# One core, attention followed by a leaky-ReLU MLP: another order of the first units of work and of three middle groups

## The chip, the cores and the metric

The kernel runs on one core of a Trainium2 chip. The metric is the device time of one execution in microseconds (us), the median of several runs. The engines are named as in the profile: PE (matrix products), DVE, ACT and POOL (elementwise work), and SP, which issues most DMAs. The profile comes from one execution, so its numbers are set against that execution's own time.

## The reference

```python
# q, k, v: (4, 8, 768, 64) float32; lam: (8,); w_in: (512, 2048) float64; w_out: (2048, 512) float64
for b in range(12):                       # blocks of 64 tokens, with a running state per head
    intra = (qb @ kb.T * Dmask) @ vb      # Dmask[i, j] = lam ** (i - j) for j <= i
    inter = (qb * lam_pow) @ kv_state
    out[block] = intra + inter
    kv_state = lam_block * kv_state + (kb * rev_pow).T @ vb
x = out as (3072, 512)
h = x @ w_in
return maximum(0.01 * h, h) @ w_out       # (3072, 512) float32
```

## The kernel before

**Precision.** Every float32 operand of a large product is split into a high, a low and a middle part (`xh`, `xl`, `xm`; `wh`, `wl`, `wm`), and a product is three passes over these parts. The weights arrive as 64-bit floats and are converted on the chip.

**Units of work.** The tokens are cut into 24 chunks of 128, and six groups of four chunks. The 2048 columns of `w_in` are cut into eight blocks `p` of 256. The list `seq` (L1030) names the work in order:

- `("a", c)`, `("b", c)`, `("r", c)`: the attention of chunk c. A round `("r", c)` (`round_of`, L556) issues on PE the transposes of chunk c+2 (until chunk 9), the outputs of chunk c, and the scores of chunk c+1; then ACT writes `xh` of chunk c, and DVE its `xl` and `xm`. DVE also masks the next scores (L478) and updates the state (L485), with POOL scaling it in between (L488). It loads k of chunk c+2, q too until chunk 9, and v. These loads of a chunk go into two buffers taken in turn, so that the loads of chunk 9 wait for the last use of those of chunk 7.
- `("wi", p)`: the conversion of block p of `w_in` (`w_in`, L650). It makes two loads of 512 KB into a ring of three buffers (`raws`), three ACT and two DVE instructions for each (L614 to L621) into one staging tile `w32`, and then `wh`, `wl`, `wm` (L629, L632, L647).
- `("up", g, p, lo, hi)`: the first layer for group g and block p (`up`, L755), limited to the chunks lo to hi where they are given. A whole unit is 24 matmuls of 512 columns in two halves, each 4 with `wh`, 4 with `wl`, and 4 with `wm`. Between the second and the third pass ACT scales the bank (L786), and after the third it writes the result to `gs` (L791).
- `("ls",)` and `("lt",)`: loads of k and q for the chunks from 10 on in strips, 16 DMAs each, those of q issued by POOL (L400).

From group 2 on, `steps` (L1038) lists the eight units of each group in the order `ORDER`, with a round after every second unit and a conversion of `w_out` after each. The last group, 5, takes the blocks from 0 to 7. After that come the products with `w_out`, most of them in a Strassen form; this part begins at about 337 us.

**What sets the order on the engines.** A planner (`Plan`, L37) goes through all operations with assumed durations and writes each engine's queue. It always takes the operation that can start first, and among those that can start at the same time the one with the lower rank; the rank is the place in `seq` (L1093), so a move in `seq` moves the priority of every operation of that unit on each engine and DMA queue. The hardware then follows the written queues in order.

The place in `seq` also fixes buffers. The halves of the units take three PSUM banks in turn:

```python
kb = ("b10", "b2")[n_b % 2] if n_b < 0 else ("b10", "b11", "b2")[(n_b + TURN_B) % 3]   # L777
```

A half waits until the half that had its bank before it, by the order of `seq`, is written out by ACT. The `gs` buffers (L760) alternate from unit to unit in the same way. For the fifth to the seventh unit of `seq` the banks are b2 and b10, b11 and b2, b10 and b11.

Some units (p below 2 in groups 0 and 1, below 6 in groups 2 and 3, below 4 in groups 4 and 5) add and subtract parts of their result on DVE (`sums`, L821) for the Strassen form. They use a scratch strip in `raws` when p is even, one in `lows` when p is odd (`spare`, L810). The others only store their result.

Of the kernel before, what the change touches and what calls it, by code (L numbers as in the profile page):

```python
# [166 lines left out]
def kernel(  # L167
# [856 lines left out]
    def add_banks(d, s):  # L1024
        for i in range(2):
# [3 lines left out]

    seq = [  # L1030
# [5 lines left out]
    nxt, n_out, begin = 3 * GC, 0, len(seq)  # L1036
    ORDER = [2, 1, 4, 3, 0, 5, 7, 6]
    steps = [(g, p) for g in range(2, NG) for p in (ORDER if g < NG - 1 else range(NP))]  # L1038

    def key_of(g, p):  # L1040
# [132 lines left out]
```

## Time and profile before

| | |
|---|---|
| median of 3 runs | 598.83 us (598.42 to 599.55) |
| profiled execution, its own time | 598.96 us |
| its span | 597.2 us |
| busy: PE, DVE, ACT, POOL | 584.0, 433.4, 306.2, 134.8 us |
| granted PE clock | 1.00 |

The profiled execution lies 0.13 us over the median, and its span 1.76 us under its own time. Busy time is an average over stages that differ: the first 100 us hold the conversions of `w_in`, the rounds until 297 us the attention, and the rest the second layer.

### The profile page before, as it was taken

How to read it: one execution, taken by the hardware profiler on the slowest of the kernel's cores; microseconds unless marked ns; L12 is line 12 of the kernel's file. 1: busy time of each engine (PE TensorE's matmuls, PEld its weight loads, DVE VectorE, ACT ScalarE, POOL GpSimd, SP SyncE). 2: the span in 40 equal slices, each digit the busy share in tenths (PEclk: the TensorE clock that was granted, in tenths of full speed). 3: DMA queues.
4: the chain of work that ended last, by engine and by line, in shares of the span. 5: the costliest groups of instructions: out<-in, count | busy, mean ns of one | idle time of the engine just before them, and what ended most of it. 6: DMA issues, size and time to landing. Idle time of an engine off the chain costs nothing.

```text
span 597.2 us, 13439 instructions
## 1 busy us (share of the span) xinstructions
PE 584.0 (98%) x5324; PEld 481.7 (81%) x5324; DVE 433.4 (73%) x596; ACT 306.2 (51%) x478; POOL 134.8 (23%) x170
## 2 busy tenths in 40 slices
PE   7899999999999999999999999999999999999997
PEld 5678888888888888888788878888888888888886
DVE  5899986525677464675269989886698887788972
ACT  4688883445555555565588783433343332335410
POOL 2654494616436436431000000000000000000000
PEclk9999999999999999999999999999999999999999
DMA  8899766978989989997889765534868668869644
GB/s 208 224 292 250 239 175 156 228 206 211 264 240 269 242 268 254 261 294 225 260 265 300 239 201 185 187 124 154 236 200 253 195 218 251 281 201 294 186 121 88
DMA packets 171199, 133.55 MB, mean 224 GB/s; under 512 B 101376, under 2 KB 147200, under 8 KB 171136
## 3 DMA queue, kind: packets, MB, share of 16 engines
q1 hardware_dynamic: 155376, 123.24, 70.8%
q10 hardware_dynamic: 13200, 5.77, 3.7%
q0 software_dynamic: 2560, 3.68, 2.4%
q8 instruction: 42, 0.69, 0.5%
q14 instruction: 21, 0.17, 0.1%
HBM read 85.99 MB, written 46.66 MB: 222 GB/s over the span
## 4 chain that ended last, share of the span: by engine, by line
PE 90%; DVE 5%; DMA 2%; ACT 1%; issue 0%; POOL 0%; SPq 0%
PE b L767 42%; PE po L909 13%; PE b L909 12%; PE psc L909 11%; PE pt L909 4%; PE po L339 3%; PE psc L339 3%; DMA attb<-in_q_dram 2%; DVE w L620 1%; DVE wm L647 1%; DVE w L621 1%; DMA attb<-in_k_dram 1%; PE pt L429 1%; DVE wl L632 0%; PE po L429 0%
## 5 line engine op out<-in xcount | busy, mean ns | idle before, releaser
L767 PE MATMUL b<-xh,wh 128*128 128x512 f32 (+2 forms) x392 | 103.5, 387 | 0.9 <-ACT xh L533 0.8
L767 PE MATMUL b<-xl,wl 128*128 128x512 f32 (+2 forms) x392 | 103.4, 387 | 0.7 <-DVE xl L534 0.6
L767 PE MATMUL b<-xm,wm 128*128 128x512 f32 (+2 forms) x392 | 103.9, 393 | 0.0
L882 ACT ACTIVATE xh<-xm 128x1024 fp32r<-128x1024 f32 x51 | 54.1, 1062 | 82.8 <-DMA xm<-b 50.3
L767 PEld LDWEIGHTS b<-xh,wh 128*128 128x128 f32 x392 | 72.8, 188 | 16.8 <-ACT xh L533 0.9
L767 PEld LDWEIGHTS b<-xl,wl 128*128 128x128 f32 x392 | 72.8, 188 | 15.9 <-DVE xl L534 1.0
L767 PEld LDWEIGHTS b<-xm,wm 128*128 128x128 f32 x392 | 71.3, 188 | 14.8
L786 ACT ACTIVATE b<-b 128x512 f32<-128x512 f32 (+2 forms) x97 | 56.2, 582 | 49.0 <-PE b L767 48.5
L791 ACT ACTIVATE gs<-b 128x512 f32<-128x512 f32 (+2 forms) x97 | 57.1, 593 | 44.0 <-PE b L767 38.2
L885 DVE SCALAR_TENSOR_TENSOR xl<-xm,xh 128x1024 fp32r<-128x1024 f32 x51 | 62.2, 1219 | 16.2 <-ACT xh L882 15.8
L889 DVE SCALAR_TENSOR_TENSOR xm<-xl,xh 128x1024 fp32r<-128x1024 f32 x52 | 63.7, 1225 | 4.0
L478 DVE TENSOR_TENSOR att<-psc,att 128x512 f32<-128x512 f32 x24 | 16.5, 688 | 38.9 <-PE psc L339 38.9
L488 POOL TENSOR_TENSOR att<-att 128x256 f32<-128x256 f32 x40 | 33.9, 847 | 42.2 <-DVE att L485 41.3
L400 POOL DMA_DIRECT2D attb<-in_q_dram x64 | 39.4, 622 | 4.9 <-DVE att L409 4.3
L449 POOL TENSOR_TENSOR att<-att 128x512 f32<-128x512 f32 (+1 forms) x20 | 24.8, 1240 | 53.7 <-PE po L339 18.9
L445 POOL TENSOR_TENSOR attb<-attb,att 128x512 f32<-128x512 f32 (+1 forms) x23 | 27.7, 1202 | 37.4 <-DMA attb<-in_k_dram 16.3
L909 PE MATMUL psc<-xm,wm 128*128 128x512 f32 x80 | 31.2, 391 | 0.8 <-DVE xm L889 0.8
L621 DVE CUSTOM_DVE_ANT_0 w<-w,lows 128x1024 uint16<-128x1024 uint16 x32 | 26.3, 822 | 7.3 <-ACT lows L618 5.9
L909 PE MATMUL psc<-xl,wl 128*128 128x512 f32 x80 | 31.2, 390 | 0.0
L909 PE MATMUL psc<-xh,wh 128*128 128x512 f32 x80 | 31.1, 389 | 0.0
L620 DVE TENSOR_SCALAR w<-w 128x512 int32<-128x512 int32 x32 | 22.1, 692 | 8.7 <-ACT w L614 8.5
L616 ACT ACTIVATE lows<-raws 128x512 uint16<-128x512 uint32 x32 | 25.2, 786 | 1.1 <-DVE w L621 1.1
(189 smaller groups left out, 1102.6 us busy)
## 6 DMA issues: line engine op xcount, KB each, us to landing
xm<-b SPq DMA_DIRECT2D x35, 512.0 KB, 4.3
b<-gs SPq DMA_DIRECT2D x24, 512.0 KB, 3.7
g<-gs SPq DMA_DIRECT2D x23, 512.0 KB, 3.6
xm<-g SPq DMA_DIRECT2D x17, 512.0 KB, 4.3
raws<-in_moe_w_in_dram SPq DMA_DIRECT2D x16, 512.0 KB, 5.2
raws<-in_moe_w_out_dram SPq DMA_DIRECT2D x16, 512.0 KB, 5.0
attb<-in_k_dram SPq DMA_DIRECT2D x48, 128.0 KB, 4.2
attb<-in_v_dram SPq DMA_DIRECT2D x24, 256.0 KB, 4.5
```

Of the source, the lines that this page charges most:

```text
L339: nc.tensor.matmul(dst[HALF[cols]], lhsT=lhsT[HALF[rows]], rhs=rhs[HALF[rows]], start=start, stop=True, skip_group_check=True)
L400: (move if nm == "k" else carry)(0.55 if nm == "k" else QSL, lambda o=o, z=z, e=nc.sync if nm == "k" else nc.gpsimd: e.dma_start(out=o.rea ...
L488: add("POOL", 0.7, lambda new=new, j=j: nc.gpsimd.tensor_tensor(state[(j + 1) % 4], new, _bc(lam_c, 2, D), op=ALU.mult), [f"st{j % 4}", "f ...
L620: add("DVE", 0.42, lambda: nc.vector.tensor_scalar(d, d, 3, None, op0=ALU.logical_shift_left), [], [key])
L621: add("DVE", 1.0, lambda: nc.vector.tensor_tensor(d, d, low, op=ALU.add), [kl], [key])
L767: nc.tensor.matmul(dst, lhsT=w[z][:, kk * 2 * P + f * P:kk * 2 * P + (f + 1) * P], rhs=x[z][:, kk, toks], start=start and kk == 0, stop=kk ...
L786: add("ACT", ns, lambda b=b: nc.scalar.activation(out=b, in_=b, func=AF.Copy, bias=0.0, scale=S + 1.0), [], [kb], rank=-1.5)
L791: add("ACT", t, lambda o=o, x=s_: nc.scalar.activation(out=o, in_=x, func=AF.Prelu, bias=0.0, scale=(1.0 + 1.0 / S) / (WS * U), alpha=0.01 ...
L882: nc.scalar.activation(out=ring[j][0], in_=g(), func=AF.Copy, bias=0.0, scale=NEAR)
L885: nc.vector.scalar_tensor_tensor(ring[j][1], g(), 1.0, ring[j][0].bitcast(F32), op0=ALU.mult, op1=ALU.subtract)
L889: nc.vector.scalar_tensor_tensor(m, l.bitcast(F32), -S, h.bitcast(F32), op0=ALU.mult, op1=ALU.add)
L909: nc.tensor.matmul(dst, lhsT=lhs(z), rhs=ring[j][z][:, col:col + n], start=first and z == 0, stop=z == 2, skip_group_check=True)
```

## The change

Only the order in two lists is changed. In `seq`, rounds 6 and 7 move ahead of units and conversions that preceded them, the eight conversions keep their order among themselves, and the units of groups 0 and 1 are sorted anew. The fifth unit is now the whole unit (0, 4) where it was the three-chunk unit (1, 5, 0, 3). For groups 2 to 4, `ORDER` names the blocks in another order. What is computed is the same; group 5 and all that follows it are listed as before.

```diff
     seq = [
            ("a", 0), ("a", 1), ("a", 2), ("a", 3), ("wi", 5), ("b", 4), ("up", 0, 5), ("wi", 2), ("wi", 6), ("r", 4), ("r", 5),
-           ("up", 0, 2), ("up", 0, 6), ("wi", 3), ("up", 0, 3), ("r", 6), ("wi", 4), ("up", 1, 5, 0, 3), ("wi", 7),
-           ("up", 0, 4), ("r", 7), ("up", 0, 7), ("wi", 0), ("up", 1, 3), ("wi", 1), ("up", 0, 1), ("ls",), ("up", 0, 0),
-           ("lt",), ("up", 1, 0), ("r", 8), ("r", 9), ("up", 1, 7), ("up", 1, 4), ("up", 1, 6), ("r", 10), ("r", 11),
-           ("up", 1, 2), ("up", 1, 1), ("up", 1, 5, 3, 4)]
+           ("up", 0, 2), ("wi", 3), ("r", 6), ("up", 0, 6), ("up", 0, 3), ("r", 7), ("wi", 4), ("up", 0, 4), ("wi", 7),
+           ("up", 1, 5, 0, 3), ("up", 1, 4), ("wi", 0), ("wi", 1), ("ls",), ("up", 0, 7), ("up", 0, 0), ("up", 0, 1), ("lt",),
+           ("up", 1, 7), ("r", 8), ("r", 9), ("up", 1, 0), ("up", 1, 3), ("r", 10), ("up", 1, 6), ("r", 11),
+           ("up", 1, 5, 3, 4), ("up", 1, 1), ("up", 1, 2)]
     nxt, n_out, begin = 3 * GC, 0, len(seq)
-    ORDER = [2, 1, 4, 3, 0, 5, 7, 6]
+    ORDER = [1, 6, 0, 3, 2, 5, 7, 4]
     steps = [(g, p) for g in range(2, NG) for p in (ORDER if g < NG - 1 else range(NP))]
```

## The prediction

> **What bounds the kernel now.** I read the share of busy time first, then the busy time by stage, since the edit touches only some stages. The columns are the window, its length, the busy time of PE, of its weight loads, of DVE, ACT and POOL with instruction counts, then clock and DMA.
>
> ```profile
> 0.00:46.00 46.00, 39.12 (x802) 30.43 (x803) 36.07 (x65) 29.46 (x51) 21.54 (x26) 1.00 0.93 242
> 46.00:100.00 54.00, 52.88 (x704) 44.07 (x704) 48.48 (x64) 40.19 (x72) 31.25 (x35) 1.00 0.73 198
> 100.00:294.00 194.00, 194.00 (x2443) 161.07 (x2441) 108.39 (x211) 103.60 (x187) 82.01 (x110) 1.00 0.89 247
> 294.00:340.00 46.00, 45.72 (x262) 37.77 (x261) 37.29 (x55) 35.80 (x60) 0.00 (x0) 1.00 0.83 268
> 340.00:362.00 22.00, 21.20 (x93) 16.94 (x92) 18.86 (x19) 16.91 (x25) 0.00 (x0) 1.00 0.74 237
> 362.00:590.00 228.00, 228.00 (x1006) 188.57 (x1005) 182.48 (x182) 80.27 (x88) 0.00 (x0) 1.00 0.65 199
> 590.00:597.20 7.20, 3.05 (x25) 2.81 (x23) 1.80 (x4) 0.00 (x0) 0.00 (x0) 0.96 0.59 121
> ```
>
> PE is the bound nearly everywhere, at full clock, and the edit neither adds nor removes a matmul. What it can change is PE's idle time: 6.88 us before 46 us, 1.12 from 46 to 100, none to 294, 0.28 to 340, 0.80 to 362, none to 590, and 4.15 in the drain. Before 46 us PE works on what stands ahead of the edit in the list (the first chunks, unit (0, 5), rounds 4 and 5), so those 6.88 us stay, and the drain too. At most 1.12 + 0.28 + 0.80 = 2.20 us can be gained, 0.37% of the time. There is no such limit on what can be lost.
>
> The 1.12 us lie in the stage where DVE, at 48.48 of 54, prepares weights and token parts just ahead of PE. I then read PE's queue in order of time there.
>
> ```profile
> 57.70 1.07 PE L767 MATMUL b<-xh,wh 128*128 128x512 f32 x4
> 58.61 1.07 PE L767 MATMUL b<-xl,wl 128*128 128x512 f32 x4
> 59.52 0.60 PE L429 MATMUL po<-att,attb 128*128 128x128 f32 x4
> ...
> 62.44 2.11 PE L767 MATMUL b<-xm,wm 128*128 128x512 f32 x8
> 64.38 0.86 PE L767 MATMUL b<-xh,wh 128*128 128x384 f32 x4
> 65.89 0.97 PE L767 MATMUL b<-xl,wl 128*128 128x384 f32 x4 [0.64 <-DVE xl L534]
> ...
> 74.06 0.60 PE L429 MATMUL po<-att,attb 128*128 128x128 f32 x4
> ...
> 77.23 0.46 PE L339 MATMUL po<-att 64*64 64x64 f32 x16 [0.34 <-DVE att L517]
> ...
> 88.73 0.69 PE L339 MATMUL po<-att,attb 64*64 64x64 f32 x32
> ```
>
> Two named waits make 0.98 of the 1.12 us: 0.64 for `xl` of chunk 6, 0.34 in round 7; 0.14 is scattered. By the list, 59.52 to 62.44 is round 6 (2.92 us), set in the middle of unit (0, 3), 64.38 starts the three-chunk unit (1, 5, 0, 3), 74.06 round 7 and 88.73 round 8. Four matmuls take 0.91 us, from start to start (58.61 - 57.70), and with 384 columns 0.68 by the ratio of columns.
>
> **Round 6 earlier: a gain.** Why was `xl` late?
>
> ```profile
> 60.82 1.28 DVE L620 TENSOR_SCALAR w<-w 128x512 int32<-128x512 int32 x1
> ...
> 62.97 1.67 DVE L629 TENSOR_SCALAR wh<-w 128x1024 fp32r<-128x1024 f32 x1
> 64.56 0.68 DVE L478 TENSOR_TENSOR att<-psc,att 128x512 f32<-128x512 f32 x1
> 65.16 0.68 DVE L534 TENSOR_TENSOR xl<-po,xh 128x512 fp32r<-128x512 f32 x1
> 65.86 0.69 DVE L536 SCALAR_TENSOR_TENSOR xm<-xl,xh 128x512 fp32r<-128x512 f32 x1
> 66.47 0.42 DVE L485 TENSOR_TENSOR att<-att,psc 128x256 f32<-128x256 f32 x1
> 66.80 1.22 DVE L632 SCALAR_TENSOR_TENSOR wl<-wh,w 128x1024 fp32r<-128x1024 f32 x1
> ...
> 68.88 1.22 DVE L647 SCALAR_TENSOR_TENSOR wm<-wl,wh 128x1024 fp32r<-128x1024 f32 x1
> ```
>
> DVE finished block 4's `wh` (1.67 us) before the operations of round 6. In the new list round 6 stands ahead of units (0, 6) and (0, 3), so it takes PE as soon as its inputs are there, k of chunk 8 last.
>
> ```profile
> 52.85 1.05 SPq L364 DMA_DIRECT2D attb<-in_k_dram  x2
> 61.74 1.07 SPq L364 DMA_DIRECT2D attb<-in_k_dram  x2
> attb<-in_k_dram SPq DMA_DIRECT2D x48, 128.0 KB, 4.2
> ```
>
> The first row is that load (issued over 1.05 us), the third the median of 4.2 us to landing: 52.85 + 1.05 + 4.2 = 58.1. So the round starts about 1.4 us sooner than 59.52, and the 1.82 us of unit (0, 3) at 57.70 run behind it. Its 2.47 us on DVE (the four rows from 64.56: 0.68, 0.68, 0.69, 0.42) then come before the end of block 4's conversion, `xl` of chunk 6 is there by about 63, and the 0.64 goes. The loads of wi3 (SP) also move up one place in rank, past nothing but a unit of PE and ACT work; I cost that at nothing, the cover being the loads' wait for a free buffer of the ring.
>
> **Unit (0, 4) as the fifth unit: a loss.** Now 64.4 us, when PE ends unit (0, 3) (the same work up to there, without a wait), is met by a unit that needs block 4's weights. With 2.47 us of round 6 ahead of it, `wh` comes at 62.97 + 1.67 + 2.47 = 67.1, or at 66.1 if it takes 0.69 as in the next rows. The cover is thin by the banks. The next unit's second half has bank b2, which (0, 4) holds first, and the seventh unit is behind (0, 4) on both banks. So only the first half of (1, 5, 0, 3) in b11 can run, once ACT has written out unit (0, 3): that takes 0.60 (row below) and about 0.2 for the end of the last matmul, so 65.2. And round 7, which now stands before wi4: its k of chunk 9, issued at 61.74, follows round 6's scores and so comes 1.4 us sooner, landing at 60.3 + 1.07 + 4.2 = 65.6.
>
> ```profile
> 64.64 0.60 ACT L791 ACTIVATE gs<-b 128x512 f32<-128x512 f32 x1 [0.33 <-PE b L767]
> 53.68 0.69 DVE L629 TENSOR_SCALAR wh<-w 128x1024 fp32r<-128x1024 f32 x1
> 50.46 0.42 DVE L620 TENSOR_SCALAR w<-w 128x512 int32<-128x512 int32 x1
> ```
>
> From 65.2 to 65.6 the half unit runs, round 7 (2.92 us) covers the rest, and PE idles from 64.4 to 65.2: 0.8 us, less 0.1 if the halves overlap: I take 0.7. The bounds are 0 (round 7 or `wh` in time) and 1.3: with no round 7 before `wl` (66.80 + 1.22 = 68.0), there are 3.6 us to fill with one `wh` group (0.91) and two groups of 384 columns (1.4).
>
> Round 7's four DVE operations, another 2.47 us, then delay wi4's last parts and wi7, which had been ahead of them; but they make chunk 7 available ten microseconds sooner, so the whole unit (1, 4) is there as cover. DVE's total is unchanged, so wi0 and wi1 end as before.
>
> **The rest of the first stage.** The 0.34 at round 7 comes from a small copy queued behind a conversion on DVE. Three such copies remain and any of them can meet the same queue; I count -0.1, between -0.34 and +0.4. Unit (0, 0) now precedes (0, 1), and needs the conversion that is done first: the scattered 0.14 shrinks by 0.1. `ls` moves up behind round 7, with its 16 DMAs on POOL and 16 on SP:
>
> ```profile
> 83.78 5.78 POOL L400 DMA_DIRECT2D attb<-in_q_dram  x10
> 60.26 1.56 POOL L445 TENSOR_TENSOR attb<-attb,att 128x512 f32<-128x512 f32 x1 [0.37 <-PE po L429]
> 62.66 1.43 POOL L449 TENSOR_TENSOR att<-att 128x512 f32<-128x512 f32 x1 [0.84 <-ACT lows L618]
> ```
>
> Ten issues take 5.78 us, 16 some 9.2, in which POOL does little of rounds 7 and 8. Round 8 came at 88.73 us, long after, so they are free; without that cover a round would wait up to 9.2 us for POOL's state scaling. SP's 16 wait for a `raws` buffer in both lists, and the weights' loads are issued before that.
>
> DVE's slow operations matter here: 1.28 for a shift that took 0.42 elsewhere began while POOL ran from 60.26 to 61.82, and 1.67 for a `wh` that took 0.69 began at 62.97 with POOL busy from 62.66 to 64.09. The Trainium skill ("SBUF — State Buffer", section "Who interferes with whom") says that such a DVE operation and a POOL operation exclude each other for a whole instruction, whichever began first. The rows agree: both ended just after POOL did. It speaks against the change, because POOL's work of round 7 and the strips now fall beside wi4 and wi7, which PE is close behind, and no longer beside wi0. From the rows one such meeting costs 0.86 or 0.98 us on DVE; I put none into the sum, since as many leave wi7 and wi0 as join wi4, and two into a rival.
>
> **The middle groups' order.** PE is busy for 194.00 of 194.00 us there, so nothing can be won. Parities show what could be lost: two users of one scratch strip stand at least two units apart in both orders, and stores alone now part the units with sums. I cost it at nothing, between 0 and the rival below.
>
> **Sum.** -0.64 + 0.7 - 0.1 - 0.1 = -0.14 us against 598.96. The median before is 598.83, so 598.7.
>
> **Rivals.** *Everything fits.* Round 7 and `wh` are in time, the new wait is zero, the whole 1.12 goes, and the shifted queues also lose the 0.28 behind 294 us: 598.83 - 1.40 = 597.4, or 596.6 with the 0.80 before 362. For it speaks that the round has a full group of units behind it sooner; against it, that the later two waits lie in work listed as before. Chance 0.25.
>
> *Block 4 late.* Slower: (0, 4) holds its banks while two POOL meetings (2 x 0.98) delay `wl` and round 7 is not ready: 1.3 + 1.96 = 3.3 of new wait, less the 0.84 won, +2.4, so 601.2; with one meeting 600.3. It decides from a new wait of 2.04 us on (1.2 over the gain). For it speak the slow rows; against it, that round 7 gives 2.92 us of cover if its k lands. Chance 0.25.
>
> *A middle group stalls.* The wait below, DVE for a scratch strip still being stored, occurs three times without hurting PE.
>
> ```profile
> DVE raws L827 <- DMA b<-raws: 7.4, 3, 5.0
> ```
>
> If its longest, 5.0, fell ahead of a chunk's `xl`, PE's cover would be one half unit (3 x 0.91 = 2.7): +2.3 and 601.0. The new order puts (2, 1) two units behind (1, 1), where they were three apart. Chance 0.10.
>
> *The queues hardly differ*, since rank breaks ties alone: 598.8. That lies within the forecast.
>
> **How the numbers follow.** The forecast, 598.7, has 0.40; its own range by the bounds is 597.7 to 599.8. Faster by more than 0.2% (1.2 us, about what a measurement of this kernel can tell from no change) is the first rival, 0.25; slower the two others, 0.35. Cutting a tenth on each side gives 597.1 to 601.2.
>
> **What would show it.** Right: PE idle from 46 to 100 us still near 1 us, but in another place; round 6's transposes at about 58 us and round 7's at 65 to 67, where they were at 74.06; no idle from 100 to 294. Wrong: PE idle of over 2 us between 64 and 72 with block 4's `wl` as releaser (slower), PE without any wait from 46 to 100 (faster), or PE idle in the middle stage.

## The result: 596.8 us, a fifth of a per cent faster

The kernel after takes 596.79 us (median of 21 runs, 595.86 to 599.62), the kernel before beside it 598.42 (21 runs, 597.44 to 599.69). The ratio is 0.9977, with a 95% interval of 0.9967 to 0.9987: 0.8 to 2.0 us less, at the edge of what can be told from no change. The forecast was 598.7 with no measurable change; the result lies below its range. The profiled execution of the kernel after took 596.75 us, its span is 594.9. Its busy time by stage, with the columns as before:

```profile
0.00:46.00 46.00, 40.20 (x809) 32.09 (x810) 37.60 (x66) 30.46 (x53) 21.44 (x26) 1.00 0.95 247
46.00:100.00 54.00, 53.78 (x710) 45.41 (x709) 42.81 (x64) 40.65 (x72) 35.09 (x40) 1.00 0.77 206
100.00:294.00 194.00, 193.72 (x2499) 160.97 (x2499) 106.74 (x211) 103.94 (x188) 78.22 (x104) 1.00 0.89 248
294.00:340.00 46.00, 46.00 (x206) 38.09 (x205) 39.41 (x58) 37.07 (x60) 0.00 (x0) 1.00 0.83 267
```

PE's idle time is now 5.80, 0.22, 0.28 and 0 us in these four stages, where it was 6.88, 1.12, 0 and 0.28. The 0.28 is one and the same wait, which has crossed the border at 294 us because all is earlier. Ahead of 46 us PE's queue is the same in both kernels; its idle time there was 5.5 to 7.1 us in the profiled executions told of below, and neither list had the shorter ones, so that the 1.08 us of difference say nothing about the edit. What the edit gained in this execution is the 0.90 us from 46 to 100: both named waits of that stretch, 0.64 and 0.34, are gone. A second execution of the same kernel has 1.11 us of idle time there, one stop without a named wait, which the last section shows.

PE's queue in order of time, kernel after:

```profile
58.10 0.60 PE L429 MATMUL po<-att,attb 128*128 128x128 f32 x4
...
61.16 2.11 PE L767 MATMUL b<-xm,wm 128*128 128x512 f32 x8
63.10 1.38 PE L767 MATMUL b<-xh,wh 128*128 128x512 f32 x4
64.32 1.09 PE L767 MATMUL b<-xl,wl 128*128 128x512 f32 x4
...
67.06 0.87 PE L767 MATMUL b<-xh,wh 128*128 128x384 f32 x4
67.77 1.09 PE L767 MATMUL b<-xm,wm 128*128 128x512 f32 x4
68.70 0.60 PE L429 MATMUL po<-att,attb 128*128 128x128 f32 x4
```

58.10 is round 6, 63.10 the start of unit (0, 4) with no named wait before it, 68.70 round 7. The other engines at that place, in one list:

```profile
61.52 1.06 ACT L627 ACTIVATE wh<-w 128x1024 fp32r<-128x1024 f32 x1 [0.39 <-DVE w L621]
62.61 1.22 DVE L632 SCALAR_TENSOR_TENSOR wl<-wh,w 128x1024 fp32r<-128x1024 f32 x1 [0.20 <-ACT wh L627]
63.76 0.68 DVE L534 TENSOR_TENSOR xl<-po,xh 128x512 fp32r<-128x512 f32 x1
```

The planner gave `wh` of block 4 to ACT (L627); before, it was DVE's, 1.67 us long (L629). It ends at 62.58, before PE has finished unit (0, 3), and DVE's next operations follow at once. `xl` of chunk 6 ends at 64.44, later than the forecast's 63, but nobody waits: unit (0, 4) reads chunks 0 to 3 only.

To compare executions whatever happened ahead of 46 us, I take the stretch from the first transposes of round 4 to the first product with `w_out`, between which all kernels do the same work. Kernel before, then kernel after:

```profile
41.41 0.60 PE L429 MATMUL po<-att,attb 128*128 128x128 f32 x4
...
336.72 0.39 PE L909 MATMUL psc<-xh,wh 128*128 128x512 f32 x1
```

```profile
39.95 0.60 PE L429 MATMUL po<-att,attb 128*128 128x128 f32 x4
...
333.82 0.39 PE L909 MATMUL psc<-xh,wh 128*128 128x512 f32 x1
```

That is 295.31 us before and 293.87 after. The same two rows give the column "stretch" below for every kernel.

### The profile page after: what moved, and what is told of

Its sections match the earlier page's. It is cut to its first block, busy times and chain, and to the rows that moved or that the text cites. A ratio compares the mean times of both kernels' runs of the same rounds, so it can differ in the third digit from the quotient of the medians.

```text
span 594.9 us, 13438 instructions
## 1 busy us (share of the span) xinstructions
PE 583.4 (98%) x5324; PEld 482.4 (81%) x5324; DVE 427.1 (72%) x596; ACT 306.4 (51%) x478; POOL 134.7 (23%) x170
## 4 chain that ended last, share of the span: by engine, by line
PE 89%; DVE 6%; DMA 2%; ACT 1%; issue 1%; DVEq 0%; ACTq 0%
PE b L767 43%; PE b L909 11%; PE po L909 11%; PE psc L909 10%; PE po L339 4%; PE pt L909 4%; PE psc L339 3%; DMA xm<-b 1%; DVE xl L885 1%; DVE wl L632 1%; PE pt L429 1%; DVE w L620 1%; DVE xm L889 1%; DMA attb<-in_k_dram 1%; DVE w L621 0%
## 5 line engine op out<-in xcount | busy, mean ns | idle before, releaser
L488 POOL TENSOR_TENSOR att<-att 128x256 f32<-128x256 f32 x40 | 35.1, 877 | 37.6 <-DVE att L485 35.3
L445 POOL TENSOR_TENSOR attb<-attb,att 128x512 f32<-128x512 f32 (+1 forms) x23 | 26.4, 1148 | 33.1 <-DMA attb<-in_k_dram 12.1
L618 ACT ACTIVATE lows<-raws 128x512 f16<-128x512 f32 x32 | 24.8, 774 | 0.0
```

What stands on the lines that cost most here:

```text
L445: lambda e="POOL": ENG[e].tensor_tensor(kr[nr], kr[nr], _bc(pow_k, 3, D)[nr], op=ALU.mult), ["fk"], [f"k{i}"])
L488: add("POOL", 0.7, lambda new=new, j=j: nc.gpsimd.tensor_tensor(state[(j + 1) % 4], new, _bc(lam_c, 2, D), op=ALU.mult), [f"st{j % 4}", "f ...
```

## The experiments

| kernel | median us (runs) | ratio to before, 95% | PE idle 46-100 | 100-294 | stretch |
|---|---|---|---|---|---|
| null | 597.61 (11) | 1.0003 [0.9993, 1.0013] | 1.07 | 0 | 294.70 |
| after_twin | 596.74 (11) | 0.9986 [0.9977, 0.9994] | 1.11 | 0.28 | 294.38 |
| after_head_dve | 597.50 (11) | 0.9996 [0.9985, 1.0007] | 1.13 | 0.28 | 295.12 |
| before_head_act | 600.61 (5) | 1.0056 [1.0043, 1.0069] | 0.58 | 1.59 | 296.39 |
| seq_only | 602.94 (6) | 1.0098 [1.0067, 1.0130] | 0 | 2.59 | 297.45 |
| order_only | 604.44 (6) | 1.0127 [1.0091, 1.0162] | 1.12 | 3.12 | 298.91 |
| r7_only | 601.43 (7) | 1.0073 [1.0044, 1.0103] | 1.25 | 1.79 | 298.88 |
| unit_only | 601.21 (12) | 1.0059 [1.0038, 1.0079] | 0.10 | 6.28 | 302.91 |
| unit_w | 599.72 (12) | 1.0033 [1.0010, 1.0057] | 0.19 | 1.46 | 295.22 |
| unit_ww | 597.99 (11) | 1.0003 [0.9994, 1.0012] | 0.20 | 0.73 | 295.31 |
| r7_w | 600.60 (12) | 1.0056 [1.0029, 1.0082] | 1.28 | 6.27 | 304.06 |
| r7_ww | 599.07 (12) | 1.0019 [1.0009, 1.0029] | 1.38 | 0.52 | 296.06 |
| seq_ww | 601.88 (6) | 1.0084 [1.0064, 1.0104] | 0.08 | 2.12 | 296.36 |
| after_w | 596.54 (11) | 0.9963 [0.9952, 0.9975] | 1.06 | 0 | 293.99 |

Idle and stretch are those of one profiled execution, the ratio is of all. The kernels with a middle stall scatter from run to run: unit_only took 598.59 to 605.75 us, and its profiled execution is the longest of these, as r7_w's is (606.59); those of unit_w (597.59), before_head_act (598.57), order_only (602.71) and seq_ww (600.95) are the shortest of theirs, so that their idle time stands for less than the ratio.

**The two lists apart.** null is the kernel before again, after_twin the kernel after again. seq_only has the new `seq` with the old `ORDER`, order_only the reverse:

```diff
 # order_only, against the kernel before
-    ORDER = [2, 1, 4, 3, 0, 5, 7, 6]
+    ORDER = [1, 6, 0, 3, 2, 5, 7, 4]
```

> The kernel before once more, as a measure of chance. Theory A (the change gains 0.9 us of PE waits between 46 and 100 us, and the other 1.1 us by which the changed kernel's profile was ahead at 46 us is chance, since the queues are the same up to there): ratio 1.000 within 0.0015, and PE idle ahead of 46 us may differ from 6.88 us by up to 1 us, with idle from 46 to 100 us again 1.1. Theory B (the two profiles differ ahead of 46 us for a reason in the kernel): idle ahead of 46 us again 6.9 within 0.2.

> The changed first list with the old order of the middle groups. Theory A (all of the gain is in the first list): ratio 0.9977 within 0.001, PE idle from 46 to 100 us 0.2 as in the changed kernel. Theory C (the middle groups' order gives a part): ratio 0.999 or more.

> The old first list with the new order of the middle groups. Theory A: ratio 1.000 within 0.001, PE idle from 46 to 100 us 1.1, none from 100 to 294. Theory C: ratio 0.999 or less. The rival of the prediction (a middle group stalls): 1.002 or more with PE idle between 100 and 294 us.

> The changed kernel once more, on the same chip as the next three. Theory A: ratio 0.998 within 0.001, PE idle from 46 to 100 us 0.2; idle ahead of 46 us anywhere between 5.8 and 7. Theory B (something in the kernel shortens the part ahead of 46 us): idle there 5.8 again.

Each list alone loses about 1%, together they gain 0.14 to 0.23%. So neither is "the" change, and `ORDER` is not free. The twin's ratio is as expected, its idle time of 1.11 us from 46 to 100 is not (0.2 was expected). With seq_only the first stage has no PE wait at all, and the middle one has this (all engines in one list):

```profile
249.43 0.43 DVE L827 TENSOR_TENSOR lows<-gs,lows 128x256 f32<-128x256 f32 x1 [3.19 <-DMA b<-lows]
...
252.05 0.60 ACT L791 ACTIVATE gs<-b 128x512 f32<-128x512 f32 x1 [4.95 <-DMA b<-gs]
...
252.70 0.80 PE L767 MATMUL b<-xh,wh 128*128 128x512 f32 x1 [2.59 <-ACT gs L791]
```

PE waits for a bank, the bank for ACT, and ACT until the buffer `gs` has been stored; DVE had stood 3.19 us for a scratch strip before that. Behind the stretch, at 360 to 363 us, both kernels also wait some 2.5 us for the second layer's inputs, where the kernel before waits 0.80.

**Block 4's first part on the other engine.** L631 offers `wh` to ACT (1.05) or DVE (0.7); here block 4 is bound to one of them.

```diff
 # after_head_dve, against the kernel after; before_head_act is the same line with ACT, against the kernel before
-        add(("ACT", "DVE"), (1.05, 0.7), head, keys, [f"wh{p}"])
+        add(*((("ACT", "DVE"), (1.05, 0.7), head) if p != 4 or late else ("DVE", 0.7, lambda: head("DVE"))), keys, [f"wh{p}"])
```

> The changed kernel, with the high part of weight block 4 held on DVE where the planner had put it on ACT (1.06 us there). Theory A1 (the high part on ACT is what keeps unit (0, 4) from waiting, the term that the prediction sized at +0.7): PE waits 0.5 to 1.0 us longer between 60 and 72 us, time 0.5 to 1.0 us above the changed kernel, ratio near 0.999. Theory A2 (the order of units alone removes the wait): no new wait, ratio 0.9977.

> The kernel before, with the high part of weight block 4 held on ACT. Theory A1 (that placement is worth the 0.64 us wait by itself): the wait for xl of chunk 6 at about 66 us goes, idle from 46 to 100 us falls from 1.1 to about 0.5, ratio 0.999, unless the shifted queues stall a middle group as the two half changes did (then over 1.005, with a PE wait of over 1.5 us between 100 and 300). Theory A3 (it needs the new order of units): the 0.64 stays.

With DVE again, the forecast's wait is there, by its size, its place and its releaser:

```profile
63.93 0.96 PE L767 MATMUL b<-xh,wh 128*128 128x384 f32 x4 [0.75 <-ACT gs L791]
```

This is the half unit of (1, 5, 0, 3) in bank b11, run in place of (0, 4), and waiting until ACT has written out unit (0, 3). DVE in the same kernel, with `wh` behind round 6:

```profile
61.32 0.68 DVE L478 TENSOR_TENSOR att<-psc,att 128x512 f32<-128x512 f32 x1
...
63.99 0.68 DVE L629 TENSOR_SCALAR wh<-w 128x1024 fp32r<-128x1024 f32 x1
```

A wait of 0.30 us for a small copy is back as well (at 86.43). The time can't be told from that of the kernel before; its interval also overlaps those of the kernel after, so it is the rows of the waits that carry the reading: with round 6 ahead on DVE, the gain hangs on `wh` being on ACT. In the kernel before the same choice shortens the first stage's idle to 0.58 us, of which 0.49 is a new wait for ACT's `xh`, and costs 0.56%. The profiled execution, the shortest of five, has stalls of 0.82 and 0.77 us in the middle.

**One move at a time.** r7_only moves round 7 ahead of ("wi", 4); unit_only exchanges unit (0, 4) with (1, 5, 0, 3).

```diff
 # unit_only, against the kernel before
-           ("up", 0, 2), ("up", 0, 6), ("wi", 3), ("up", 0, 3), ("r", 6), ("wi", 4), ("up", 1, 5, 0, 3), ("wi", 7),
-           ("up", 0, 4), ("r", 7), ("up", 0, 7), ...
+           ("up", 0, 2), ("up", 0, 6), ("wi", 3), ("up", 0, 3), ("r", 6), ("wi", 4), ("up", 0, 4), ("wi", 7),
+           ("up", 1, 5, 0, 3), ("r", 7), ("up", 0, 7), ...
```

> The kernel before with round 7 alone moved ahead of wi4. Theory A: round 7 comes about 5 us sooner, its 0.34 us wait may go, the 0.64 us wait at (1, 5, 0, 3) stays, since it comes earlier: idle from 46 to 100 us 0.7 to 1.1. Theory D (the middle groups have no slack for any shift of the queues): a PE wait of over 1 us between 100 and 300 us, ratio over 1.003.

> The kernel before with the fifth unit alone exchanged: (0, 4) ahead of (1, 5, 0, 3), round 7 left behind both. Theory A: the 0.64 us wait for xl of chunk 6 goes, and since the high part stays on DVE behind round 6, a new wait of 0.7 us or more for block 4's weights comes at about 64 us, as the prediction had it: idle from 46 to 100 us 1 to 2. Theory A2 (the exchange alone gives the gain): idle 0.2 to 0.5. Theory D: again a PE wait of over 1 us between 100 and 300 us.

The exchange alone removes both waits of the first stage (idle 0.10 us), with round 6 left where it was. The wait of 0.7 us that was expected did not come, although `wh` of block 4 is on DVE here: it stands ahead of round 6's operations, not behind them, and ends at 63.36, when PE has just finished unit (0, 3).

```profile
61.69 1.67 DVE L629 TENSOR_SCALAR wh<-w 128x1024 fp32r<-128x1024 f32 x1
63.28 0.68 DVE L478 TENSOR_TENSOR att<-psc,att 128x512 f32<-128x512 f32 x1
...
63.41 2.82 PE L767 MATMUL b<-xh,wh 128*128 128x512 f32 x12
```

But it stalls in the middle. All engines in one list:

```profile
231.90 0.42 DVE L827 TENSOR_TENSOR lows<-gs,lows 128x256 f32<-128x256 f32 x1
...
233.22 2.19 SPq L400 DMA_DIRECT2D raws<-in_k_dram  x1
...
238.21 0.64 SPq L835 DMA_DIRECT2D b<-lows  x1
...
245.14 0.43 DVE L827 TENSOR_TENSOR lows<-gs 128x256 f32<-128x256 f32 x1 [10.83 <-DMA b<-lows]
...
247.33 0.15 DVE L517 COPY att<-po 128x2 f32<-128x2 f32 x1
...
247.54 0.71 PE L339 MATMUL po<-att 64*64 64x64 f32 x16 [6.28 <-DVE att L517]
```

DVE filled the strip by 232.3. SP issued its store only at 238.21, behind the loads of strips and weights in its queue; it landed at 245.05, and the next unit's first operation waited for it until 245.14. Queued behind that on DVE is the small copy L517, for which a round on PE waits. r7_only has the same chain (DVE 6.34 us, PE 1.79 at 243.81), and it keeps two waits in the first stage, 0.38 us for `xl` of chunk 6 and 0.68 for a small copy.

**Is it the strip's store?** The queues are kept, and the stores of the strip read another tile, so that the next unit need not wait for them. In the first form they read the unit's own `gs`:

```diff
 # keep() in sums(), L835: unit_y, r7_y, after_y
-            move(0.4 * n, lambda: nc.sync.dma_start(out=d[:, k:k + n], in_=x), [key], ...
+            move(0.4 * n, lambda: nc.sync.dma_start(out=d[:, k:k + n], in_=y.rearrange("p f h t -> p (f h) t")[:, :n] if key == "low1" else x), [key], ...
```

> Unit (0, 4) exchanged alone, with the same queues on every engine, but the stores from the odd blocks' scratch strip in lows read the unit's own result in gs instead: as many bytes, issued at the same place, so that DVE never waits until the strip is stored (what is stored there is then not the Strassen sums). If that wait is what stalls the middle stage: DVE's wait of 10.83 us at 245.14 and PE's 6.28 at 247.54 are gone, PE is idle for under 0.6 us from 100 to 294, and the time falls from 601.2 to between 596.5 and 598. If transfers feed that stage late whatever DVE waits for: a PE wait of 2 to 6 us remains between 217 and 256 us with another releaser (a chunk's loads, or ACT at gs, which is now read by one store more), and the time stays at 600 to 602.

> Round 7 moved alone, with the same exchange of the source of the stores from the strip in lows (what is stored there is not the Strassen sums). If DVE's wait for the strip's store is the cause: its wait of 6.34 us at 241.41 and PE's 1.79 at 243.81 are gone, the waits of 0.38 and 0.68 near 64 and 72 us stay, and the time falls from 601.4 to about 598, the time of the kernel before. If not: 600 to 602, with a wait of 1 to 3 us left between 217 and 256.

> The kernel after with the same exchange of the source (what is stored there is not the Strassen sums). Here PE does not wait in the middle stage, so if only PE's waits count it gains nothing: 596.8, ratio to the kernel after within 0.1%. If the strips' stores cost time in a way that PE's waits do not show, it would be faster than the kernel after by 0.2% or more, 595.5 or less; if the later release of gs hurts, slower, with ACT waiting for gs.

All three became slower: 614.27, 613.15 and 608.39 us, ratios 1.0265 [1.0239, 1.0291], 1.0267 [1.0246, 1.0289] and 1.0190 [1.0166, 1.0214]. DVE's waits for `b<-lows` are gone, but `gs` is now held until these stores have landed too. The waits from 100 to 294 us in after_y (total, times, longest):

```profile
ACT gs L791 <- DMA b<-gs: 16.0, 4, 4.4
...
PE b L767 <- ACT gs L791: 7.0, 4, 2.1
```

In the kernel after the first of these is 0.8 us in two waits. Holding `gs` longer costs more than holding the strip, since PE's banks wait behind it.

So this form says nothing about the strip as the cause. In the second form the stores read `wh`, which nothing writes in that stage: for the strip in `lows` alone (unit_w, r7_w, after_w), then for both strips (unit_ww, r7_ww, seq_ww).

```diff
 # unit_ww, r7_ww, seq_ww; in unit_w, r7_w and after_w the condition is key == "low1"
+            ... in_=W[p][0].bitcast(F32)[:, :n * HT].rearrange("p (i t) -> p i t", i=n) if key in ("low1", "zr") else x ...
```

> Unit (0, 4) exchanged alone, with the same queues on every engine, but the stores from the odd blocks' scratch strip in lows read the block's weights wh instead, which nothing writes in that stage: as many bytes, issued at the same place, so that neither DVE nor ACT waits for these stores (what is stored is not the Strassen sums). If DVE's wait for the strip is what stalls the middle stage: its wait of 10.83 us at 245.14 and PE's 6.28 at 247.54 are gone, PE is idle for under 0.6 us from 100 to 294, and the time falls from 601.2 to between 596.5 and 598. If transfers feed that stage late whatever DVE waits for: a PE wait of 2 to 6 us remains between 217 and 256 us with another releaser, and the time stays at 600 to 602.

> Round 7 moved alone, with the stores from the strip in lows reading wh instead (what is stored is not the Strassen sums). If DVE's wait for the strip's store is the cause: its wait of 6.34 us at 241.41 and PE's 1.79 at 243.81 are gone, the waits of 0.38 and 0.68 near 64 and 72 us stay, and the time falls from 601.4 to about 598, that of the kernel before. If not: 600 to 602, with a wait of 1 to 3 us left between 217 and 256.

> The kernel after with the stores from the strip in lows reading wh instead (what is stored is not the Strassen sums). PE does not wait in the middle stage of the kernel after, so if only PE's waits count nothing is gained: 596.8, within 0.1% of the kernel after. If the strip's stores cost time that PE's waits do not show, 595.5 or less.

Freeing one strip settled little: the other took its place. unit_w took 599.72 us where 596.5 to 598 was expected, with DVE waiting 3.9 us for the store from `raws`. r7_w, all engines in one list:

```profile
247.04 0.42 DVE L827 TENSOR_TENSOR raws<-gs,raws 128x256 f32<-128x256 f32 x1 [7.54 <-DMA b<-raws]
...
248.58 0.71 PE L339 MATMUL po<-att 64*64 64x64 f32 x16 [4.81 <-DVE att L517]
```

after_w's interval overlaps that of the first comparison (0.9967 to 0.9987) and lies just below the twin's (0.9977 to 0.9994); its stretch is no shorter (293.99 against 293.87 and 294.38). The kernel after has these waits on DVE from 100 to 294 us:

```profile
DVE lows L827 <- DMA b<-lows: 12.3, 4, 5.1
```

Where PE does not wait behind them, 12.3 us of waits on DVE cost nothing in the stretch, and by the ratios a few tenths of a per cent at most.

> Unit (0, 4) exchanged alone, same queues, with the stores of both scratch strips (lows and raws) reading the weights wh (what is stored is not the Strassen sums). With the strip in lows alone freed, DVE's next wait of 3.94 us was for the store from raws, and PE still waited 1.22. If the strips' stores are the whole cause: no DVE wait for b<-lows or b<-raws, no PE wait over 0.5 us from 100 to 294, no run above 600, median 597.0 to 598.3, that is 0.997 to 1.000 of the kernel before. If another store or load takes their place (gs, or the strips of k): PE waits of 1 to 5 us remain, some runs at 602 to 604 as in unit_w, median 599 or more.

> Round 7 moved alone, same queues, stores of both strips reading wh (what is stored is not the Strassen sums). In r7_w DVE's wait of 7.54 us for the store from raws, and PE's of 4.81 behind it, stood where the strip in lows had been. If the strips' stores are the whole cause: those are gone, the two early waits of 0.4 to 1.2 us stay, median 597.5 to 598.8, 0.999 to 1.001 of the kernel before, no run above 600. If not: median 600 to 601 again, with a PE wait behind ACT at gs or a chunk's loads.

> The new seq with the old ORDER, same queues, stores of both strips reading wh (what is stored is not the Strassen sums). There PE's 2.59 us at 252.70 stood behind ACT, which waited 4.95 us for the store from gs, and that store came after DVE's 3.19 us for the strip in lows. If the strip started it: both waits shrink to under 1 us and the time falls from 602.9 to 597 to 599. If the store from gs is late by itself: ACT's wait of 4 to 5 us and PE's of 2 to 3 stay, and the time stays at 601 to 603.

With both strips freed, unit_ww falls from 1.0059 to 1.0003 and r7_ww from 1.0073 to 1.0019, and no run of unit_ww is above 599.4. The intervals with and without the strips' waits do not overlap in either pair. DVE's waits for `b<-lows` and `b<-raws` are gone in both. PE's waits from 100 to 294 us in unit_ww:

```profile
PE po L339 <- ACT att L517: 0.7, 1, 0.7
```

So for these two the strips' stores are the cause of the stall, shown with unchanged queues. They are nearly all of it, not the whole as expected: unit_ww keeps the wait above, where none over 0.5 us was expected, and r7_ww, expected at 1.001 at most with no run above 600, is at 1.0019 with one at 600.26. The kernel before with both strips freed was not run, so what that does without a stall is known only from after_w, for one strip. seq_ww is the miss: 1.0098 to 1.0084, intervals that overlap, and the wait for `gs` is still there without any strip before it:

```profile
237.35 4.80 SPq L400 DMA_DIRECT2D raws<-in_k_dram  x6
...
238.42 0.41 DVE L827 TENSOR_TENSOR gs<-gs 128x256 f32<-128x256 f32 x1
...
244.72 0.52 SPq L835 DMA_DIRECT2D b<-gs  x1
...
250.59 0.60 ACT L791 ACTIVATE gs<-b 128x512 f32<-128x512 f32 x1 [4.28 <-DMA b<-gs]
251.24 1.19 PE L767 MATMUL b<-xh,wh 128*128 128x512 f32 x4 [1.92 <-ACT gs L791]
```

There the store from `gs` is late by itself: DVE had last written that buffer by 238.83, SP issued the store at 244.72, behind six loads of strips among others, and it landed at 250.49. Both are buffers that are released by a store, and a store waits its turn in SP's queue. What stalls order_only and before_head_act was not tested in this way, and a second queue for the stores was not tried.

## Why the prediction was wrong

**What bounds the kernel: right, with a hole.** PE's idle time is what the edit could change, and the gain stayed below the bound of 2.20 us. "There is no such limit on what can be lost" was the more important half: five edits that each make a part of the change, or a choice it brought, lost 0.56 to 1.27%, most of it in the stage where PE had no idle time. A stage that is busy for 194.00 of 194.00 us has no idle time to win; the view does not say how much slack its buffers have.

**Round 6 earlier: the gain came, not by this step.** The round did not move against PE's other work: it follows the same matmuls as before, and its 1.42 us (59.52 to 58.10) were there at round 4 already (41.41 and 39.95, 1.46). By the planner's code rank breaks ties only, and the higher rank changed nothing in PE's queue here. That 58.10 is the forecast's 58.1 is luck. The 0.64 us for `xl` of chunk 6 went because the fifth unit does not read that chunk, as unit_only shows.

**Unit (0, 4) as the fifth unit, +0.7: the step that failed.** The size was right (0.75 us in after_head_dve) and so were the place and the bank. Its premise was not: that block 4's `wh` comes on DVE behind round 6's 2.47 us. In the kernel after, ACT makes it from 61.52 to 62.58, and the wait is zero. The forecast carried an engine over from the trace of before, where the code offers a choice of two. The planner's reason is not shown: with (0, 4) as the fifth unit alone it kept DVE, put `wh` ahead of round 6, and PE did not wait either. One reading is off beside that: of the seventh unit's banks, b10 is behind (0, 4), but b11 is behind the sixth unit; the term does not rest on it. Without that term its own sum is -0.84 us; PE's idle time fell by 0.90, the twin was 0.84 us faster (0.4 to 1.4), the first comparison 1.4 (0.8 to 2.0). That they come so close is in part luck: of the other terms the copies were counted at -0.1 where 0.34 went, and the scattered 0.14 us, counted to shrink by 0.1, was 0.22. The measured time also lies only 0.3 us below the range, while the kernel before, run beside it, came out 0.41 us under the 598.83 that the forecast starts from. As for the stretch, it is 0.92 us shorter by the means of two executions of the queues of before and three of those of after (295.01 against 294.08, after_w counted among the latter).

**Round 7, 65 to 67 us expected:** 68.70; most of (0, 4) ran ahead of it, without a wait. The copies' 0.34 us went, within the term's bounds. For POOL's strips and the slow DVE operations beside POOL, PE did not wait: block 4's `wh` avoided DVE.

**The middle order, "cost it at nothing":** its result is right for the pair of lists and its reasoning wrong. By parity no two users of a strip come close; what decided in unit_only and r7_only is when SP issues the stores and how long they take to land. The new order alone costs 1.27%.

**The rivals.** "Everything fits" (597.4 forecast) happened in its main part: the new wait was zero and both named waits went, since ACT had `wh` in time. The 0.28 us behind 294 us that it also counted on did not go, and neither did the 0.80 before 362. "Block 4 late" did not happen: no PE wait for `wl`. "A middle group stalls" did not happen to the kernel after, but it is what happened to the five mixtures, at 600.6 to 604.4 us where it gave 601.0, and in unit_only and r7_only by its mechanism (a copy for PE stood behind the wait, not a chunk's `xl`). Why this pair of lists escapes is known only as far as the rows go: DVE waits 12.3 us for `b<-lows` there, against 15.0 in r7_only and 19.6 in unit_only, but with no copy for PE queued right behind these waits. No run shows a rule by which one could tell such a pair from the lists alone.

## What to carry over

Before costing a move in a planned schedule, look for every operation that the code offers to more than one engine: the trace shows only the choice that was taken. Where an edit to the first stage changes a queue that a planner writes, expect its effect in the stage with no idle time, at buffers that a store must release. To show that such a buffer is the cause, let the store read something else and keep the queues; but look first at what that something else then holds up.

## What the runs showed of the hardware

A short stall can cost twice. In r7_w the clock fell to half during PE's wait of 4.81 us and stayed there after it (columns: window, its length, five engines, granted clock, DMA):

```profile
247.00:248.00 1.00, 0.00 (x0) 0.00 (x0) 0.96 (x3) 0.07 (x1) 0.00 (x0) 0.50 0.42 67
...
252.00:253.00 1.00, 1.00 (x4) 0.81 (x3) 0.56 (x3) 0.00 (x0) 0.50 (x1) 0.50 1.15 254
253.00:254.00 1.00, 1.00 (x4) 0.76 (x4) 1.00 (x3) 0.00 (x0) 0.92 (x2) 0.61 0.77 108
254.00:255.00 1.00, 1.00 (x6) 0.83 (x5) 1.00 (x2) 0.58 (x1) 0.98 (x1) 1.00 0.67 161
```

The same kernel's PE queue behind the wait:

```profile
249.22 2.07 PE L767 MATMUL b<-xm,wm 128*128 128x512 f32 x4
...
254.19 1.07 PE L767 MATMUL b<-xh,wh 128*128 128x512 f32 x4
```

Between these starts lie 12 matmuls of 512 columns. They took 4.97 us where 3 x 0.91 = 2.73 are usual, so 2.2 us are lost on top. In windows of 1 us the clock also fell after the wait of 1.79 us in r7_only (0.66, 0.50, 0.50, 0.64 from 245) and at the end of that of 2.59 in seq_only (0.67, 0.50, 0.50, 0.63 from 252), and stayed at 1.00 through those of 1.92 in seq_ww and 2.45 in order_only. The length of the wait alone does not decide. A window's mean tells how much of it ran at half clock, (1 - 0.66) / 0.5 = 0.68 us for the first; summed up, half clock lasted 3.4 us in r7_only, 3.4 in seq_only and 6.8 in r7_w. The Trainium skill ("TensorE: Matmul & The Clock Gate", Part 1) tells of a free-running window of about 3.4 us that has to pass idle. The 3.4 us and twice 3.4 us agree; that 1.79 us without a matmul were enough does not.

In three executions with both new lists PE stops inside unit (0, 4) without a releaser in the trace. after_twin:

```profile
62.46 0.39 PE L767 MATMUL b<-xh,wh 128*128 128x512 f32 x1
63.96 0.86 PE L767 MATMUL b<-xh,wh 128*128 128x512 f32 x3 [1.11 <-issue]
```

It is 1.11 us here, 0.79 in after_w and 0.82 in after_y; in the kernel after the four matmuls of that place take 1.38 us, 1.07 elsewhere. r7_w, whose list is that of before but for round 7, has 1.22 us of it at 64.94; seq_only and seq_ww, with the new `seq` too, have none. What PE waits for there is open; it is why the idle time of after_twin from 46 to 100 us is no smaller than before, though the named waits are gone.
